# Shorter zero matmuls in three pauses of the head, and a new written-out order, in a fused attention and MLP kernel

## The chip, the cores and the metric

The kernel runs on one core of a Trainium2 chip. The metric is the device time of one execution in microseconds (us). The profiler also gives the span of a profiled execution, from its first to its last recorded instruction or transfer. Engines are named as in the profile: PE (TensorE matmuls), PEld (its weight loads), DVE (VectorE), ACT (ScalarE), POOL (GpSimd) and SP (SyncE, which issues nearly all DMAs here).

## The reference, cut to what matters

A transformer block on one sequence of S = 2048 tokens of width D = 448, in bf16. Six modulation vectors come from a condition vector; attention has 16 heads of 28 channels, and each query sees 8 keys at a stride of 2 tokens; the MLP is 1792 wide.

```python
mod = (silu(c) @ w_mod).reshape(1, 6, 1, 448)
sa, ca, ga, sb, cb, gb = (mod[:, i] for i in range(6))
h = layernorm(x) * (1 + ca) + sa
x = x + ga * (local_attention(h, wqkv) @ wo)      # 8 keys, dilation 2
h = layernorm(x) * (1 + cb) + sb
y = layernorm(h)
x = x + gb * (gelu(y @ w1 + b1) @ w2 + b2)
```

## The kernel before, in words

The tokens are split into two streams (even and odd, so that the dilated window becomes a dense one), and into 8 blocks `p` of 128 rows by 2 streams. A block is normalised on DVE, transposed (by PE for blocks 0 to 3, task names `tr0` to `tr3`; by DMA for 4 to 7, `zT4` to `zT7`), and scaled into `hT`. Blocks are projected to Q and K in units `[0] [1] [2,3] [4,5] [6,7]` (tasks `qk0`, `qk1`, `qk2`, `qk4`, `qk6`, each in halves `_0` for Q and `_1` for K and pieces `a` and `b`). Attention goes in nine batches `i` of 114 queries: V projection `v`, logits `lt`, exp on ACT, a mask multiply on DVE, denominators `pd`, weighted values `po`, a division on DVE (`omul`). Then per block an output projection `wo`, two layernorms on DVE, a DMA transpose `yT`, and per pair of blocks an MLP with tasks `w1`, gelu on ACT, `w2`, a final addition `fin` on DVE and a store.

Every step is a task with a number, added by `add` to a `Plan`. Nothing is scheduled while the kernel runs: `ORDER`, a text of 677 entries, gives the order in which the tasks are emitted, and so the order of instructions in each engine's own stream, which each engine executes strictly in that order. An entry `83:A` puts task 83 on ACT, `:D` on DVE, `:P` on POOL; `:R` picks the other way of a PE task, in which the quarter-depth matmuls (64 rows deep, line 534) come first and the full-depth ones (line 528) last. `SLOTS` gives each buffer its place; the four PSUM places (2 banks each) are reused all the time, so that a PE task also waits for the engine that reads the place's previous content. SP's loads keep one fixed order among themselves.

An entry `53+11@53` calls `filler(11, task 53)` ahead of task 53: that many matmuls of zeros on PE (line 370), written to the PSUM place that task 53 will overwrite. There are four such entries in the order before: ahead of 53 (`c_cols`, which turns the condition vector into columns), 69 (`mod_cols`), 85 and 91 (first pieces of `qk0`).

Numbers used below: 68 is `tr0`, 106 `tr1`, 128 `tr2`, 138 `tr3`, 164 `v0`, 209 `v1`, 114 and 115 the pieces of `qk1_1`, 111 and 112 those of `qk1_0`, 151 `mods` (line 599), 173 `po0`. On the other engines: 119 to 132 are statistics of blocks 2 and 3 (lines 433 and 435), 177 to 190 of blocks 4 and 5, 244 to 257 of blocks 6 and 7; 125, 126, 135, 136 the normalisations of blocks 2 and 3 (line 453); 107 to 110 the evictions of `tr1` into `hT` (lines 477 and 479); 165 and 210 the evictions of `v0` and `v1` (line 678 on ACT, 681 on DVE); 168 and 171 the masks of batch 0 (line 708); 663, 667, 671 and 675 the last additions (line 849) and 664, 668, 672 and 676 their stores.

Of the kernel before, what the change touches and what calls it, by code (L numbers as in the profile page):

```python
# [14 lines left out]
S, D, H, DH, F = 2048, 448, 16, 28, 1792  # L15
# [26 lines left out]
ENGINE = {"A": "ACT", "D": "DVE", "P": "POOL", "R": "PE2"}  # L42
RATE = 310e3
SLOTS = [
# [5 lines left out]
]  # L50
ORDER = """
0 4 16 1 2 3 8 17 14 13 15 18 9 6 19 11 12 7 20 5 10 21 61 53+11@53 22 59 23 54 62 60 55 63 56 57 64 58 65 66 24 67 25
68+14@69 69 26 27 77 71 70 28 72 78 73 74 29 76 75 85+9@85 82 86 30 97 80:A 31 91+3@91 92 83:A 99 93 32 84:A 98 81:A
79 94 100 95:R 101 33 129 102 87 103 88 96 104 89:R 34 131 105 35 121 106 90 36 132 164 130 122 119 37 109:A 133 108
134 110 169 107 165 166 120 38 136 209 123 254 170 124 256 167 135 39 114 257 125 255 137 244 115:R 126 245 40 210:D
127 138 116 128 258 189 259 111 141:A 41 246 112:R 190 139:A 171 168 140:A 42 151 247 261 113 248 179 43 249 173 142
152 44 214 180 260 211 45 251 215 148 250 177 262 46 212 216 153 263 178 252:A 187 172 276 181 174 150:D 182 175 253
188 184 143 191 183 213 277 176 185 192 218 186 145:D 217 147 219 194 193 47 220 195 154 144:R 48 149 221 196 311
146:D 266:A 49 265 117 50 264 278 312 118 313 51 267 281 279 528 52 272 564 282 157 280 314 529:R 159 274 155 283 269
199:A 156 200:A 315 198:A 161 222 271 162 163 530 197 284 160 285 286 419 202 223 287 158 201:R 288 204 226 289 224  # L60
203 227 225 228 229 205 290 231 293 206:R 207 230 294 291 232 316 208 292 346 233 295 317 236 296 234 351 347 318 348
268 298 349 235 297 237 299 352 350 320 270 300 319 273 238 353 321 301 239 303 322 354 302 241 420 304 275 240 305
323 242 306 356 243 355 455 421 324 307 308 357 309 310 456 381 358 325 359 457 326 328 397 327 360 329 382:R 361 398
363 399 362 330 364 331 365 366 387 333 384 367 368 383 332 369 385 334 386 370 335 392:R 390 373 400 401 389 336 388
374 338 404 391 337 371 403 339 372 340 375 422 396 408 376 393 395 341 394 406 377 418 343 342 378 409 405 379:A
344:A 380 423 402 425 461 426 458 345 424 407 459 427 414 462 410 463 411 415 460 465 464 428 466 412 430 413 467 431
565 468 491 416 429 507 566 417 432 492:R 509 508 469 495 496 493 433 470 494 510 514 471 497 511 473 434 513 474 472
435 512 437 502:R 436 475 438 500 476 439 498 440 499 501 478 442 441 477 515 505 443 503 479 444 504 517 480 506 447
527 483 516 481 484 445 531 570 482 448 532 534 446 485 518 449 486 571 533 523 535 487 572 536 524 519 450 537 488
520 538 452 539 451 567 489:D 453:D 521 490 568 540 569 454 522 541 573 574 525 575 542 576 526 616 600 543 577 601:R  # L70
618 544 617 546 545 547 548 549 578 550 603 551 602 552 604 606 619 623 579 605 622 582 580 620 583 581 584 553 611:R
607 585 556 609 554 610 621 557 555 608 558 587 586 559 626 612 588 615 560 614 632 589 613 561 590 562:A 627 592 563
591 593 594 624 595 597 596 625 598 599 633 628 630 629 631 651 634 635 641:R 652 653 636 645 644 643 642 646:R 637
638 654 656 640 639 658 655 661 647 649 657 650 659 648 662 660 665 663 664 666 669 667 670 668 673 671 672 674 675
676
"""


# [73 lines left out]
def kernel(  # L152
# [14 lines left out]
    nc = tc.nc  # L167
# [56 lines left out]
    warm_w = cst.tile([128, 256], BF16, name="warm_w")  # L224
# [142 lines left out]
    def filler(n, t):  # L367

        for _ in range(n):
            nc.tensor.matmul(t.sums[0].t[:, 0, 0:256], lhsT=warm_w[:, 0:128], rhs=warm_w[:, 0:256], start=True, stop=True)  # L370


    psc = psum("ps_c")
# [490 lines left out]
    for pi, (batches, tiles) in enumerate(PHASES):  # L864
# [18 lines left out]
        if pi < len(PHASES) - 1:  # L883
            tbl = add("ACT", 1.28, lambda: nc.scalar.preload_act_table_set(EXP_SET), after=list(gelus), name="tbl")
    P.emit(filler)

# [28 lines left out]
```

## Time and profile before

| | |
|---|---|
| median of 3 runs (lowest, highest) | 172.77 us (172.54, 174.36) |
| the profiled execution, its own time | 172.62 us |
| its span | 170.6 us |
| PE busy | 165.6 us (97%) |
| DVE busy | 115.7 us (68%) |
| ACT busy | 104.9 us (62%) |
| POOL busy | 42.0 us (25%) |
| matmuls recorded | 2152, of these 37 of zeros |

Rows of a chain or timeline begin with the start and the duration in us. A row that merges several instructions (x6) gives the time from the first start to the last end. What stands in brackets is the idle time of the engine just ahead of the row, and what ended it. Matmul durations are latencies: consecutive ones overlap, so the distance between two starts is shorter than one duration. Rows of groups give the total busy time and the mean of one instruction in ns.

### The profile page before, as it was taken

How to read it: one execution, taken by the hardware profiler on the slowest of the kernel's cores; microseconds unless marked ns; L12 is line 12 of the kernel's file. 1: busy time of each engine (PE TensorE's matmuls, PEld its weight loads, DVE VectorE, ACT ScalarE, POOL GpSimd, SP SyncE). 2: the span in 40 equal slices, each digit the busy share in tenths (PEclk: the TensorE clock that was granted, in tenths of full speed). 3: DMA queues.
4: the chain of work that ended last, by engine and by line, in shares of the span. 5: the costliest groups of instructions: out<-in, count | busy, mean ns of one | idle time of the engine just before them, and what ended most of it. 6: DMA issues, size and time to landing. Idle time of an engine off the chain costs nothing.

```text
span 170.6 us, 4990 instructions
## 1 busy us (share of the span) xinstructions
PE 165.6 (97%) x2152; PEld 84.3 (49%) x2152; DVE 115.7 (68%) x289; ACT 104.9 (62%) x144; POOL 42.0 (25%) x64
## 2 busy tenths in 40 slices
PE   7989999999999999999999999999999999999993
PEld 5856564453445454435555343555534455444562
DVE  6687999799989969897445168966689952200041
ACT  3278688679947995758939455866772920258200
POOL 6003132300011220499000057030018620007200
PEclk9999999999999999999999999999999999999999
DMA  5999999998000033000740100006600034100011
GB/s 157 317 319 316 261 244 291 156 259 248 6 0 4 6 62 67 0 0 0 63 121 0 58 0 0 0 4 88 147 4 2 0 65 115 56 0 0 0 58 54
DMA packets 20708, 15.12 MB, mean 89 GB/s; under 512 B 13705, under 2 KB 19726, under 8 KB 20686
## 3 DMA queue, kind: packets, MB, share of 16 engines
q1 hardware_dynamic: 20684, 14.80, 36.1%
q8 instruction: 17, 0.28, 0.7%
q14 instruction: 5, 0.04, 0.1%
q10 hardware_dynamic: 2, 0.00, 0.0%
HBM read 9.81 MB, written 1.84 MB: 68 GB/s over the span
## 4 chain that ended last, share of the span: by engine, by line
PE 86%; DMA 7%; DVE 2%; SPq 2%; issue 0%
PE p L843 25%; PE p L528 22%; PE pq L528 11%; PE pw L760 7%; DMA x_all<-in_A_x_dram 4%; PE p L534 4%; PE lt L695 3%; PE po L728 3%; DMA wm_st<-in_w_mod_dram 3%; PE pv L528 3%; PE pv L663 3%; PE pq L534 2%; PE pd L717 1%; DVE stt L433 1%; SPq L329 1%; SPq L325 1%
## 5 line engine op out<-in xcount | busy, mean ns | idle before, releaser
L821 ACT ACTIVATE hm<-p,b_col 128x512 bf16<-128x512 f32 x56 | 34.4, 687 | 30.0 <-PE p L534 23.1
L843 PE MATMUL p<-w_s,hm 128*128 128x448 bf16 (+1 forms) x238 | 43.8, 342 | 0.0
L528 PE MATMUL p<-yT,w_s 128*128 128x512 bf16 x168 | 38.6, 380 | 0.0
L843 PEld LDWEIGHTS <-hm 128*128 128x128 bf16 x238 | 22.8, 98 | 19.1 <-issue 0.3
L449 POOL TENSOR_TENSOR rs_all<-tv_all,neg_half 128x2 f32<-128x2 f32 x22 | 15.8, 724 | 60.9 <-DVE tv_all L447 54.1
L528 PEld LDWEIGHTS <-w_s 128*128 128x128 bf16 x168 | 15.7, 98 | 20.9 <-issue 3.4
L849 DVE TENSOR_TENSOR x_all<-p,x1p 128x896 bf16<-128x896 f32 (+2 forms) x10 | 9.0, 902 | 23.9 <-PE p L843 23.9
L528 PE MATMUL pq<-hT,Wqk 128*128 128x512 bf16 (+1 forms) x108 | 22.6, 345 | 0.4 <-DVE vb L681 0.4
L433 DVE BATCH_NORM_STATS2 stt<-x_all 128x6 f32<-128x448 bf16 x32 | 18.6, 613 | 2.1 <-DMA x_all<-in_A_x_dram 1.9
L702 ACT ACTIVATE et<-lt 128x928 bf16<-128x928 f32 x18 | 16.0, 946 | 1.2 <-PE lt L695 1.2
L798 POOL TENSOR_TENSOR x1p<-x_all,gbb_bc 128x448 f32<-128x448 bf16 x16 | 16.6, 1064 | 0.1
L708 DVE TENSOR_TENSOR et<-et,mask 128x928 bf16<-128x928 bf16 x18 | 11.2, 634 | 4.9 <-ACT et L702 4.9
L745 DVE TENSOR_TENSOR qT<-po,den 128x912 bf16<-128x912 f32 x9 | 10.0, 1106 | 6.6 <-ACT den L739 5.2
L528 PEld LDWEIGHTS <-Wqk 128*128 128x128 bf16 x108 | 9.4, 97 | 9.9 <-issue 3.5
L760 PE MATMUL pw<-wo_s,qT 128*128 128x448 bf16 x64 | 13.3, 353 | 0.0
L737 ACT ACTIVATE den<-pd 128x928 f32<-128x928 f32 x9 | 8.5, 954 | 7.8 <-PE pd L717 7.8
L767 DVE TENSOR_TENSOR x_all<-pw,x_all 128x896 bf16<-128x896 f32 x8 | 8.6, 1081 | 6.8 <-PE pw L760 6.8
L825 POOL COPY seen<-hm 128x1 bf16<-128x1 bf16 x4 | 3.2, 788 | 34.9 <-ACT hm L821 34.9
L776 DVE TENSOR_TENSOR h<-h,mod_bc 128x896 bf16<-128x896 bf16 x16 | 10.3, 672 | 0.1
L588 ACT CAST kT<-pq 128x1024 bf16<-128x1024 f32 x7 | 7.1, 1011 | 4.5 <-PE pq L528 2.4
L739 ACT ACTIVATE den<-den,den_bias 128x928 f32<-128x928 f32 x9 | 9.5, 1069 | 0.2
L433 DVE BATCH_NORM_STATS2 stt<-h 128x6 f32<-128x448 bf16 x16 | 9.2, 610 | 0.0
(101 smaller groups left out, 186.3 us busy)
## 6 DMA issues: line engine op xcount, KB each, us to landing
wmod<-in_w_mod_dram SPq DMA_DIRECT2D x4, 392.0 KB, 10.7
w_s<-in_B_w_dram SPq DMA_DIRECT2D x7, 224.0 KB, 5.2
out_dram<-x_all SPq DMA_DIRECT2D x7, 224.0 KB
x_all<-in_A_x_dram SPq DMA_DIRECT2D x3, 448.0 KB
w_s<-in_B_w_dram SPq DMA_DIRECT2D x3, 448.0 KB, 4.3
wqk_st<-in_A_wqkv_dram SPq DMA_DIRECT2D x3, 225.0 KB
wm_st<-in_w_mod_dram SPq DMA_DIRECT2D x1, 588.0 KB
x_all<-in_A_x_dram SPq DMA_DIRECT2D x2, 224.0 KB
```

The lines of the kernel that those rows point to most:

```text
L433: add("DVE", 0.53, lambda: nc.vector.bn_stats(out=stt[:, w, b, :], in_=src()), reads=reads, bufs=bufs, after=early if w == b == 0 else (), ...
L449: add("POOL", 0.55 + 0.17 * n, lambda: nc.gpsimd.tensor_tensor(out=r, in0=tv, in1=neg_half[:, 0:n], op=ALU.pow), reads=[f"tv{w}_{b0}", "ne ...
L528: nc.tensor.matmul(out(), lhsT=lhs(kt, slice(0, 128)), rhs=rhs(kt, slice(0, 128)), start=first and kt == 0, stop=not first and kt == KT - 2)
L534: nc.tensor.matmul(out(), lhsT=lhs(KT - 1, rows), rhs=rhs(KT - 1, rows), start=first, stop=not first, tile_position=(rows.start, 0))
L702: exps.append(add("ACT", 0.83, lambda half=half, lt=lt: nc.scalar.activation(out=et.t[:, 2 * half:2 * half + 2].rearrange("p r m c -> p r ...
L708: nc.vector.tensor_tensor(out=ev, in0=ev, in1=mask[:], op=ALU.mult)
L745: nc.vector.tensor_tensor(out=qT[:, :, LEAD + q00:LEAD + q00 + 2 * WQ], in0=po.t[:, :, 0:NS * 4 * WQ].rearrange("p j (m c) -> p m j c", c=WQ),
L760: nc.tensor.matmul(pw.t[:, s, 0:D], lhsT=qT[:, NS * PLACE[ft] + s, LEAD + 128 * p:LEAD + 128 * p + 128], rhs=wo_s[:, ft, :], start=(ft == ...
L776: add("DVE", 0.55, lambda vec=vec, op=op: nc.vector.tensor_tensor(out=h2.t[:], in0=h2.t[:], in1=vec.unsqueeze(1).to_broadcast([128, NS, D] ...
L798: add("POOL", 1.0, lambda n=n: nc.gpsimd.tensor_tensor(out=x1p.t[:, n, :], in0=xn(p, n), in1=gbb2_bc[:], op=ALU.add), reads=[f"x{p}", "gbb ...
L821: gelus.append(add("ACT", 0.585, lambda f=f, a=a, p1=p1s[g]: nc.scalar.activation(out=hm.t[:, f].rearrange("p n c -> p (n c)"), in_=p1.t[: ...
L843: nc.tensor.matmul(p2.t[:, n, 0:c1 - c0], lhsT=hm.t[:, f, n, q * 128:(q + 1) * 128], rhs=w2_s[:, f, c0:c1], start=(f == parts[0][0]), stop ...
```

## The change

The zero matmuls get 128 columns in place of 256. They stand ahead of tasks 53 (20 in place of 11), 69 (19 in place of 14) and 85 (18 in place of 9); the 3 ahead of task 91 are gone: 57 in place of 37, with 7296 columns in place of 9472. `ORDER` and `SLOTS` are new as a whole. The set of tasks is the same; 95 changes of the array's mode along PE's stream become 91 (mode: rows by columns of the tile that a matmul uses, as full, 64x128, 128x64 or 64x32). Of the diff, the heads and the ends of the order:

```diff
-0 4 16 1 2 3 8 17 14 13 15 18 9 6 19 11 12 7 20 5 10 21 61 53+11@53 22 59 23 54 62 60 55 63 56 57 64 58 65 66 24 67 25
-68+14@69 69 26 27 77 71 70 28 72 78 73 74 29 76 75 85+9@85 82 86 30 97 80:A 31 91+3@91 92 83:A 99 93 32 84:A 98 81:A
-79 94 100 95:R 101 33 129 102 87 103 88 96 104 89:R 34 131 105 35 121 106 90 36 132 164 130 122 119 37 109:A 133 108
-134 110 169 107 165 166 120 38 136 209 123 254 170 124 256 167 135 39 114 257 125 255 137 244 115:R 126 245 40 210:D
-127 138 116 128 258 189 259 111 141:A 41 246 112:R 190 139:A 171 168 140:A 42 151 247 261 113 248 179 43 249 173 142
...
-638 654 656 640 639 658 655 661 647 649 657 650 659 648 662 660 665 663 664 666 669 667 670 668 673 671 672 674 675
-676
+0 4 16 1 2 13 8 17 14 15 18 3 9 6 19 12 7 20 11 5 10 21 61 53+20@53 22 59 23 54 62 60 55 63 56 57 64 58 66 65 24 67 25
+68+19@69 69 26 27 77 71 70 28 72 78 75 74 29 76 73 82 30 85+18@85 86 99 83:A 31 91 80:A 92 97 32 93 84:A 100 81 94 98
+79 95:R 101 33 119 102 87 103 88 96 104 89:R 34 121 105 35 129 106 90 36 122 164 120 130 131 37 108:A 187 109:A 132
+123 110 169 124 165 107 166 38 256 209 170 126 246 167 257 39 133 177 114 134 210 179 168 115:R 40 135 125 111 116 189
+127 136 112:R 41 190 247 137:A 254 138 188 180 113 255 178 128 191 171 42 151 181 192 139:A 140 43 142 173 141:A 182
...
+654 646:R 657 653 652 656 640 658 655 665 650 649 647 659 648 669 661 670 662 671 672 660 673 663 666 664 674 667 675
+668 676
...
-            nc.tensor.matmul(t.sums[0].t[:, 0, 0:256], lhsT=warm_w[:, 0:128], rhs=warm_w[:, 0:256], start=True, stop=True)
+            nc.tensor.matmul(t.sums[0].t[:, 0, 0:128], lhsT=warm_w[:, 0:128], rhs=warm_w[:, 0:128], start=True, stop=True)
```

More of the change, by code (lines that the diff above doesn't have):

```diff
@@ L56 @@
-127 138 116 128 258 189 259 111 141:A 41 246 112:R 190 139:A 171 168 140:A 42 151 247 261 113 248 179 43 249 173 142
[L57 to L70, printed above, removed]
@@ L71 @@
-618 544 617 546 545 547 548 549 578 550 603 551 602 552 604 606 619 623 579 605 622 582 580 620 583 581 584 553 611:R
-607 585 556 609 554 610 621 557 555 608 558 587 586 559 626 612 588 615 560 614 632 589 613 561 590 562:A 627 592 563
-591 593 594 624 595 597 596 625 598 599 633 628 630 629 631 651 634 635 641:R 652 653 636 645 644 643 642 646:R 637
-638 654 656 640 639 658 655 661 647 649 657 650 659 648 662 660 665 663 664 666 669 667 670 668 673 671 672 674 675
-676
+0 4 16 1 2 13 8 17 14 15 18 3 9 6 19 12 7 20 11 5 10 21 61 53+20@53 22 59 23 54 62 60 55 63 56 57 64 58 66 65 24 67 25
@@ new lines @@
+68+19@69 69 26 27 77 71 70 28 72 78 75 74 29 76 73 82 30 85+18@85 86 99 83:A 31 91 80:A 92 97 32 93 84:A 100 81 94 98
+79 95:R 101 33 119 102 87 103 88 96 104 89:R 34 121 105 35 129 106 90 36 122 164 120 130 131 37 108:A 187 109:A 132
+123 110 169 124 165 107 166 38 256 209 170 126 246 167 257 39 133 177 114 134 210 179 168 115:R 40 135 125 111 116 189
+127 136 112:R 41 190 247 137:A 254 138 188 180 113 255 178 128 191 171 42 151 181 192 139:A 140 43 142 173 141:A 182
+244 44 214 152 258 245 211 193 45 215 311 184 183 153 194 212 46 216 47 172 248 259 195:A 312:D 185:A 143 174 249 186
@@ new lines @@
+175 213 144:R 260 145 250 176 196 218 251 261 217 252:A 146:D 148 219 253 262:D 220 147:R 150:D 263 221 117 276 149
+118 197 199:A 154 200 48 198 281 49 277:D 278 282 201 50 51 419 279 283 52 264 266:A 205:R 280 203 156 265:A 155 284
+285 158 207 222 157 286 160 161 267:A 202 162 287 223 528:A 269:R 288 204 224 289 226 271 225 159 227 163 272 290 228
+293 229 346 274 291 294 231 230 316 292 347 232 313 206 295 233 314 296 236 317 234 273:R 208 297 235 237 298 238 315
+348 299 275 351 268 318 349 300 239 352 303 319 301 529 270 350 241 321 302 353 320 455 530 354 304 240 355 305 356
@@ new lines @@
+242:D 306 420 243 322 308 307 357 456:R 323 309 310 421 564 324 358 381 457:D 359 325 397 360 326 382:R 361 399 327
+328 398 362 363 329 364 330 365 331 387 366 385 383 333 368 386 367 332 384 369 334 392:R 388 370 391 335 373 400 389
+401 338 390 374 371 403 339 406 336 394 405 372 337 375 396 340 393 408 402 395 341 418 422 425 404 461 423 409 342
+462 343 424 412 426 344 463 345 376 414 427 377 428 378 429 379:D 430 380 413 431 458 415 459 432 407 460 416 464 465
+410 466 417 433 411 467 502 491 434 468 437 435 492:R 438 506 436 439 505 440 503 441 504 442 443 497 444 495 494 447
@@ new lines @@
+496 445 448 493 446 449 450 565:R 498 510 513 501 500 469 451 452 566 512 453:A 507 499 511 454 470 514 473 521 509
+471 508 474 472 475 527 476 534 570 567 478 523 535 477 479 571 536 531 568 480 524 572 532 483 522 569 484 533 573
+525 574 575 538 481 537 526 576 515 482 485 486 539 577 516 540 487 488 517 600 541 489:A 578 490 542 579 580 518 582
+581 543 606 519 544 520 546 545 583 601:R 547 584 607 548 585 608 549 610 609 587 551 550 586 616 603 552 602 588 553
+605 611:R 589 618 554 619 617 622 590 604 592 621 556 620 593 591 632 555 557 613 594 558 615 595 612 630 559 614 596
@@ L76 @@
+597 633 561 560 623 562:A 626 563 598 599 624 625 631 627 634 641 628 635 629 636:R 644 642 645 643 651 638 637 639
+654 646:R 657 653 652 656 640 658 655 665 650 649 647 659 648 669 661 670 662 671 672 660 673 663 666 664 674 667 675
+668 676
 """
```

10 rows, old and new, of the table SLOTS are left out of this document.

## The prediction

> **What bounds the kernel now.** I read the page first, then the chain that ended last, then the timeline of the first 25 us by engine. The page:
>
> ```profile
> span 170.6 us, 4990 instructions
> PE 165.6 (97%) x2152; PEld 84.3 (49%) x2152; DVE 115.7 (68%) x289; ACT 104.9 (62%) x144; POOL 42.0 (25%) x64
> PE 86%; DMA 7%; DVE 2%; SPq 2%; issue 0%
> ```
>
> PE is busy 97% of the span and makes up 86% of the chain. The windows say where PE ever runs dry and how full DVE is there (columns of the windows: length, then busy time with the instruction count for PE, PEld, DVE, ACT and POOL):
>
> ```profile
> 18.00:22.00 4.00, 3.58 (x38) 2.51 (x36) 4.00 (x13) 2.55 (x4) 1.32 (x3) 1.00 1.02 239
> 26.00:40.00 14.00, 14.00 (x253) 6.08 (x251) 12.86 (x27) 10.92 (x15) 2.17 (x4) 1.00 1.14 238
> 40.00:60.00 20.00, 20.00 (x341) 9.02 (x338) 19.23 (x45) 16.51 (x20) 2.39 (x3) 1.00 0.10 33
> ```
>
> In 18 to 22 PE is idle for 0.42, then in the whole of 26 to 60 for nothing, and the list of waits has none of PE behind 22 either. So a new order can shorten that stretch only by making PE's own stream shorter, and can lengthen it by any single late input. The chain, with the head's longest piece and the last ones:
>
> ```profile
> 9.84 7.61 DMA x_all<-in_A_x_dram
> 17.48 1.15 DVE stt L433 x2
> 18.63 0.30 DVE zy L453
> 18.93 0.09 DVE mvs L435
> ...
> 167.66 0.39 DVE x_all L849
> ```
>
> The last step is an addition on DVE (block 7). In the head the end is set by a load of x (blocks 6 and 7), which lands at 17.46, then by DVE's list behind it, statistics, normalisations and the eviction of `v1`.
>
> **The zero matmuls.** They stand in gaps that other things end:
>
> ```profile
> 1.12 2.53 PE L370 MATMUL ps_c<-warm_w 128*128 128x256 bf16 x11 [1.12 <-DVE warm_w L240]
> 4.02 2.38 PE L370 MATMUL ps_col<-warm_w 128*128 128x256 bf16 x14
> 6.24 0.61 PE L510 MATMUL ptr<-ident,zy 128*128 128x128 bf16 x8
> 6.68 1.32 PE L398 MATMUL ps_col<-silu_bc,wm_st 112*128 112x32 bf16 x40
> 7.93 1.16 PE L370 MATMUL pq<-warm_w 128*128 128x256 bf16 x9
> 8.92 0.60 PE L550 MATMUL pq<-hT,Wqk 128*128 128x256 bf16 x4
> L370 PE MATMUL ps_c<-warm_w x11: 393/421/421, 1.1 to 3.2; 128*128 128x256 bf16 x11
> L370 PE MATMUL pq<-warm_w x12: 272/272/283, 7.9 to 9.6; 128*128 128x256 bf16 x12
> ```
>
> The first eleven start at 1.1 to 3.2, so 0.21 us apart for 256 columns, 0.107 us for 128: twenty of 128 take 2.1 us, 0.2 less than eleven of 256. The nine of the third pause take from 7.93 to 8.92, 0.11 us each; eighteen of 128 at half of that, 0.055, take the same 1.0 us. The nineteen take between 1.05 us (all at 0.055) and 2.0 us (all at 0.107) where fourteen took 2.2. So all three groups end with or ahead of the ones before, and what ends the pauses is not theirs: the condition vector, the normalised block 0, the scaled block 0. The three dropped stood between the first pieces of `qk0`, in a pause that ends with DVE's copy of the K weights. Cost and gain of this part: 0; bounds -0.1 (if the third group held `qk0` up) and the price of a slow clock (second rival).
>
> [...] The row: one zero matmul takes 421 ns at first and 272 ns in the last pauses. [...]
>
> **The mode changes.** Their price is read where the same six matmuls stand with and without one ahead:
>
> ```profile
> 40.77 1.29 PE pq L528 x6
> 42.07 0.32 PE pq L534 x2
> ...
> 46.28 0.54 PE pq L534 x4
> 46.82 1.40 PE pq L528 x6
> ```
>
> Six full ones behind others of full mode take 1.29, behind 64-row ones 1.40. Two 64-row ones cost 0.32, four cost 0.54, so 0.22 for two and 0.10 for the change. Four changes fewer (95 to 91, all of it between `tr1` and the first `w1`, 55 to 51, and one fewer and one more later): 4 x 0.1 = -0.4 us. Bounds: -0.45 and 0, the latter if PE waits there anyway.
>
> **The head.** The new stream of PE behind `tr1` is `v0`, `lt0`, `v1`, `qk1_1`, `qk1_0`, then `tr3`, `tr2`, `mods`; before, the transposes stood ahead of `qk1_0`. The eviction of `v1` goes from DVE to ACT. On DVE, statistics of blocks 4 and 5 (187) and 6 and 7 (256) come earlier, 187 even ahead of the evictions 110 and 107 that `v1` needs. The rows of before:
>
> ```profile
> 9.21 1.10 SPq L329 DMA_DIRECT2D x_all<-in_A_x_dram  x2
> 11.63 0.63 DVE L433 BATCH_NORM_STATS2 stt<-x_all 128x6 f32<-128x448 bf16 x1 [0.38 <-DMA x_all<-in_A_x_dram]
> 14.62 1.05 DVE L477 TENSOR_SCALAR hT<-ptr,mod_col 128x256 bf16<-128x256 bf16 x3
> 16.29 1.64 PE L663 MATMUL pv<-Wv,hT 128*64 128x448 bf16 x16
> 17.86 0.83 PE L528 MATMUL pq<-hT,Wqk 128*128 128x256 bf16 x6
> 19.61 1.29 PE L510 MATMUL ptr<-ident,zy 128*128 128x128 bf16 x16
> 21.32 0.82 PE L528 MATMUL pq<-hT,Wqk 128*128 128x256 bf16 x6 [0.42 <-DVE vb L681]
> 23.15 0.94 PE L599 MATMUL pb<-wmod,silu_bc 112*32 112x448 bf16 x16
> Wv<-in_A_wqkv_dram SPq DMA_DIRECT2D x1, 336.0 KB, 5.3
> x_all<-in_A_x_dram SPq DMA_DIRECT2D x3, 448.0 KB
> ```
>
> When x of blocks 4 and 5 lands no row says. Between the landing of blocks 2 and 3 (11.63) and of 6 and 7 (17.46), SP's order has the V weights (336 KB and two small pieces, together some 450 KB), blocks 4 and 5 (448 KB), blocks 6 and 7 (448 KB). Three equal shares of 5.83 us put it at 15.5, an estimate; bounds 14.6 (it makes nobody wait) and 17.46.
>
> DVE's list is the same work as before up to 14.6 (the statistics of blocks 2 and 3 and two normalisations, in another order), then the wait to 15.5, 187 to 16.05 (0.53 each when back to back: 1.15 for two, less the overlap), a small pair 0.15, two evictions at 1.05/3 = 0.35 each: 16.9. So `v1` starts at 16.95 in place of 16.29: 0.65 late. `v1` takes 1.57 (16.29 to 17.86), `qk1_1` 1.75 (17.86 to 19.61), `qk1_0` 1.83 (21.32 to 23.15): PE is at 22.1 then. `tr3` needs 136, the last normalisation. Ahead of it behind 17.48 stand five statistics (2.65), four normalisations (0.29 each, 1.16), two small ones (0.16) and a mask (0.56): 22.0, and its tail copy on ACT (0.3) ends at 22.35. `tr3` and `tr2` take 0.95 (16 of 0.055 and the issue): `mods` starts at 23.35 in place of 23.15. The waits of before (0.42 for the eviction, 0.3 inside the transposes) are gone, two others stand in their place. Term: +0.2. Bounds: -0.2 (DVE's list 0.4 faster; then `qk1_0` ends last), +1.5 (x at 17.46: 187 to 18.0, then 0.85, and the list of 4.5 behind that: 23.4, `tr3` at 23.7, `mods` at 24.65).
>
> Nothing is behind that to absorb or add: up to `omul` of batch 4, DVE loses an eviction of `v1`, one of `qk2`, a few of `hT` (3.5 us together) and gains the evictions of `v2` and `v3` and some of `hT` (3.6 us): 0.
>
> **The tail.** Before, the last piece of PE is followed by one addition and its store. In the new order the addition of block 7's first stream (667) comes with only a 6-matmul piece behind its inputs, so two additions and two stores end together.
>
> ```profile
> L849 DVE TENSOR_TENSOR x_all<-p,x1p 128x448 bf16<-128x448 f32 x1 | 0.6, 625 | 1.6 <-PE p L843 1.6
> 166.74 1.67 SPq L853 DMA_DIRECT2D out_dram<-x_all  x2
> 166.79 0.83 PE L843 MATMUL p<-w_s,hm 128*128 128x224 bf16 x7
> ```
>
> The piece takes some 0.57 (6 of the 0.1 at which the last 7 follow each other, within 0.83), the addition 0.625: 0.1 late; SP then issues two stores behind each other, the first while the last addition (0.39) runs. By the row of the last two issues, 1.67 with a wait for the last addition in it, one issue is between 0.4 and 0.8, so the last store waits 0 to 0.4 more for its turn. Term +0.2; bounds 0 and +0.5.
>
> **The sum.** 172.62 (the profiled execution's own time: span 170.6 and 2.0 around it) + 0 - 0.4 + 0.2 + 0.2 = 172.6, no change. The median of the runs is 172.77, 0.15 above that execution; the forecast for a median is 172.8. Its own range by the bounds, which do not all fall together: 172.0 to 174.0.
>
> **Rivals.**
>
> First, slower: DVE is late for `po0`. From 17.48 the new list holds, up to and with the second mask of batch 0 (171), six statistics, four normalisations, nine small ones and two masks. With overlap (0.53, 0.29, 0.08, 0.56) that is 6.2 us, done at 23.7, and `po0` is due at 24.2. The means of the groups are longer:
>
> ```profile
> L433 DVE BATCH_NORM_STATS2 stt<-x_all 128x6 f32<-128x448 bf16 x32 | 18.6, 613 | 2.1 <-DMA x_all<-in_A_x_dram 1.9
> L708 DVE TENSOR_TENSOR et<-et,mask 128x928 bf16<-128x928 bf16 x18 | 11.2, 634 | 4.9 <-ACT et L702 4.9
> L435 DVE BATCH_NORM_AGGREGATE mvs<-stt 128x2 f32<-128x6 f32 x48 | 7.3, 168 | 0.0
> L453 DVE TENSOR_SCALAR zy<-x_all,mvs,rs_all 128x448 bf16<-128x448 bf16 x16 | 5.6, 379 | 0.1
> ```
>
> Without overlap, by these means, the list is 8.0 us, done at 25.5: 1.3 late, and the evictions 140 and 142, which `lt1` and `v3` need, come behind it. It decides from 0.5 us of lateness on. For it: DVE is full from 18 to 22 and 96% full from 40 to 60. Against it: the chain shows the overlap (0.30 and 0.09 where the means say 0.38 and 0.17). With 0.2 more for the tail: 172.8 + 1.6 = 174.4. Chance 0.20.
>
> Second, slower: the clock. If PE stays at half rate past 6.2 us, `tr0` takes twice its 0.4 (6.24 to 6.68) and the modulation columns up to twice their 1.3 us (6.68 to 7.95): 0.4 to 1.7 late, 173.2 to 174.5. [...] Chance 0.06.
>
> Third, faster: the load of x lands early and DVE's list keeps ahead, so that both of the head's new waits vanish (another 0.6) and the tail costs nothing (0.2): 172.8 - 0.2 - 0.6 - 0.2 = 171.8; with the mode changes costing a little more, 171.5. It can't be much more, since PE has only 0.4 of idle time behind 11 us. For it: the order before lost its time at just this load. Against: the wait at 17.46 stands in both. Chance 0.12.
>
> **How the numbers follow.** The forecast has 0.62, the rivals 0.20, 0.06 and 0.12. 1% of 172.77, about what a measurement of this kernel can tell from no change, is 1.73: 171.04 and 174.50. Slower by more: 0.09 from the first rival, 0.03 from the second, 0.08 from the forecast's upper bound where DVE or the load is later than worked out: 0.20. Faster by more: a third of the third rival, and little else: 0.06. Within: 0.74. The range takes in both rivals' times: 171.4 to 174.8.
>
> **What would show it.** `v1` starting 0.4 to 0.9 late with a wait for DVE ahead; `mods` at 23.2 to 23.6; PE without idle time from there to its end; PE's stream from `mods` to its last matmul 0.4 shorter; the end 0.2 longer behind the last matmul. Wrong if PE shows idle time over 0.3 us behind 25 us, or if the mean of the third pause's matmuls shows the slow clock.

## The result, and the profile after

| | us |
|---|---|
| changed kernel, median of 4 runs (lowest, highest) | 175.31 (175.2, 175.5) |
| kernel before, beside it, median of 4 runs | 173.0 (172.54, 174.36) |
| ratio, with its 95% interval | 1.0109 [1.0062, 1.0157] |
| the profiled execution: its own time, its span | 175.34, 173.6 |
| forecast (range) | 172.8 (171.4 to 174.8) |

The change is slower by 1.1%, and the time lies above the range: the medians are 2.3 us apart, the two profiled executions 2.7 (172.62 and 175.34). The kernel before varied between 172.1 and 177.7 on the chips used later, so experiments are compared by their ratio to the runs of it on the same chip; runs in which the chip was in a slower state are left out of the ratios (five of the ten of e2 and five of the twelve of f2 among them), and the profiles of f1 and h3 fell in it.

The page of the changed kernel; of the queues, q8 is taken for the one of TensorE's instructions, since its 17 packets fit their number (below):

```profile
span 173.6 us, 5023 instructions
PE 165.4 (95%) x2172; PEld 84.9 (49%) x2172; DVE 118.3 (68%) x291; ACT 105.3 (61%) x146; POOL 42.4 (24%) x60
q8 instruction: 17, 0.28, 0.7%
PE 82%; DMA 10%; DVE 4%; issue 1%; SPq 1%
```

PE's busy time is 0.2 us less than before (165.6), the span 3.0 us longer: PE now stands idle, which the prediction excluded behind 22 us. Four of the eight rows of PE's waits in the changed kernel (what PE waited for, total, count, longest); the other four lie ahead of 18 us:

```profile
PE pd L717 <- issue: 1.5, 1, 1.5
PE pw L760 <- DVE w_s L617: 0.6, 1, 0.6
PE ptr L510 <- DVE zy L453: 0.4, 1, 0.4
PE pq L370 <- DVE mod_col L410: 0.3, 1, 0.3
```

The longest has "issue" as its cause: no semaphore, no engine and no transfer that the profile shows. The timeline of PE around it, in the changed kernel:

```profile
112.97 2.44 PE L843 MATMUL p<-w_s,hm 128*128 128x448 bf16 x12
115.35 0.39 PE L717 MATMUL pd<-et,ones_k 64*32 64x464 bf16 x8
115.55 1.29 PE L728 MATMUL po<-et,vb 64*32 64x57 bf16 x128
116.66 0.38 PE L717 MATMUL pd<-et,ones_k 64*32 64x464 bf16 x3
118.53 0.38 PE L717 MATMUL pd<-et,ones_k 64*32 64x464 bf16 x5 [1.49 <-issue]
118.84 4.33 PE L843 MATMUL p<-w_s,hm 128*128 128x448 bf16 x22
```

and of the same batches in the kernel before:

```profile
116.33 0.39 PE L717 MATMUL pd<-et,ones_k 64*32 64x464 bf16 x8
116.54 0.73 PE L728 MATMUL po<-et,vb 64*32 64x57 bf16 x64
117.20 0.44 PE L695 MATMUL lt<-qT,kT 28*64 28x58 bf16 x32
117.58 2.82 PE L843 MATMUL p<-w_s,hm 128*128 128x448 bf16 x14
120.33 0.39 PE L717 MATMUL pd<-et,ones_k 64*32 64x464 bf16 x8
120.54 0.73 PE L728 MATMUL po<-et,vb 64*32 64x57 bf16 x64
```

The new order has `pd8`, `po8`, `po7` and `pd7` in one run of 144 short matmuls, with as many weight loads, in 1.5 us; before, long `w2` matmuls stood in between. In the midst of `pd7`, whose eight matmuls have the same inputs ready, PE stops behind the third. Eight matmuls of `pd` take 0.20 us from start to start (115.35 to 115.55), 0.025 each, so the third starts at 116.71; the fourth starts at 118.53, **1.8 us** late. (The 1.49 in brackets is counted from the modelled end of the third.) The DMA transfers of two adjoining stretches of the changed kernel, 115 to 115.9:

```profile
DMA packets 0, 0.00 MB, mean 0 GB/s; under 512 B 0, under 2 KB 0, under 8 KB 0
```

and 115.9 to 118.6 (queue, packets, MB, share of 16 engines):

```profile
q8 instruction: 1, 0.02, 2.4%
```

A packet of PE's instructions is fetched there. The trace has it from 115.97 to 117.02, so PE goes on 2.6 us behind its start and 1.5 us behind its end; what happens between the end of the transfer and PE's next matmul no view shows. The page counts 17 such packets for 4344 matmuls and weight loads, some 256 instructions each.

TensorE's last matmul, one of `w2`, starts 2.9 us later than before. How much of that lies where is read from the `w2` matmuls (min, median and max duration in ns, then first and last start), before:

```profile
L843 PE MATMUL p<-w_s,hm x238: 259/352/363, 78.3 to 167.4; 128*128 128x448 bf16 x105, 128*128 128x224 bf16 x14
```

and after:

```profile
L843 PE MATMUL p<-w_s,hm x238: 259/352/363, 78.8 to 170.3; 128*128 128x448 bf16 x105, 128*128 128x224 bf16 x14
```

From first to last it was 89.1, it is 91.5: **+2.4**, of which the stop is 1.8. Ahead of it, PE's timeline of the changed kernel has `v1`, `mods` and the first `wo`:

```profile
17.70 1.64 PE L663 MATMUL pv<-Wv,hT 128*64 128x448 bf16 x16
22.77 1.06 PE L510 MATMUL ptr<-ident,zy 128*128 128x128 bf16 x16
23.75 0.56 PE L599 MATMUL pb<-wmod,silu_bc 112*32 112x448 bf16 x8
42.82 1.69 PE L760 MATMUL pw<-wo_s,qT 128*128 128x448 bf16 x8 [0.59 <-DVE w_s L617]
```

`mods` is 0.6 late (23.15 before), and `wo0` waits 0.6. From `mods` to the first `w2` it was 55.15, it is 55.05: without that wait 0.7 shorter than before, and the 0.6 of the 2.4 that the stop doesn't explain is mostly work that the new order has moved behind the first `w2`: 32 more matmuls of `lt` (256 against 224) stand there, and the new order without a stop, below, has 0.5 more in this stretch.

### The profile page after: what moved, and what is told of

Read it like the earlier page. It is cut to its first block, busy times and chain, and to the rows that moved or that the text cites. A ratio compares the mean times of both kernels' runs of the same rounds, so it can differ in the third digit from the quotient of the medians.

```text
span 173.6 us, 5023 instructions
## 1 busy us (share of the span) xinstructions
PE 165.4 (95%) x2172; PEld 84.9 (49%) x2172; DVE 118.3 (68%) x291; ACT 105.3 (61%) x146; POOL 42.4 (24%) x60
## 3 DMA queue, kind: packets, MB, share of 16 engines
HBM read 9.81 MB, written 1.84 MB: 67 GB/s over the span
## 4 chain that ended last, share of the span: by engine, by line
PE 82%; DMA 10%; DVE 4%; issue 1%; SPq 1%
PE p L843 25%; PE p L528 21%; PE pq L528 9%; PE pw L760 7%; PE p L534 4%; DMA x_all<-in_A_x_dram 4%; DMA mod_bc<-mod_hbm 3%; DMA wm_st<-in_w_mod_dram 3%; PE lt L695 3%; PE pv L528 3%; PE pv L663 3%; PE po L728 3%; PE pq L534 2%; PE pd L717 2%; DVE stt L433 1%
## 5 line engine op out<-in xcount | busy, mean ns | idle before, releaser
L843 PE MATMUL p<-w_s,hm 128*128 128x448 bf16 (+1 forms) x238 | 44.3, 342 | 0.0
L449 POOL TENSOR_TENSOR rs_all<-tv_all,neg_half 128x2 f32<-128x2 f32 x22 | 17.8, 816 | 84.4 <-DVE tv_all L447 84.3
L453 DVE TENSOR_SCALAR zy<-h,mvs,rs_all 128x448 bf16<-128x448 bf16 x16 | 8.5, 567 | 3.9 <-POOL rs_all L449 3.8
L776 DVE TENSOR_TENSOR h<-h,mod_bc 128x896 bf16<-128x896 bf16 x16 | 9.4, 620 | 0.1
```

What stands on the lines that cost most here:

```text
L449: add("POOL", 0.55 + 0.17 * n, lambda: nc.gpsimd.tensor_tensor(out=r, in0=tv, in1=neg_half[:, 0:n], op=ALU.pow), reads=[f"tv{w}_{b0}", "ne ...
L843: nc.tensor.matmul(p2.t[:, n, 0:c1 - c0], lhsT=hm.t[:, f, n, q * 128:(q + 1) * 128], rhs=w2_s[:, f, c0:c1], start=(f == parts[0][0]), stop ...
```

## The experiments

What separates the theories is **which** of the change's parts is slower: the order, the short zero matmuls, or only both together. "The stretch" below is from the first to the last start of a `w2` matmul (89.1 before, 91.5 after); the expectations count to the last one's end, 0.2 to 0.3 more.

**The parts alone, first set.** The new order with the old zero matmuls, the old order with the new ones, and the new order with 37 short ones. In these three the second group stands behind `tr0`, ahead of 69, while in both kernels it stands ahead of task 68, which is `tr0`, and writes the place of 69 (so the line on the four entries, above, is to be read). The first set is therefore not quite the parts alone; the second is.

```diff
-61 53+20@53 ... 68+19@69 69 ... 85+18@85 ... 31 91 80:A
+61 53+11@53 ... 68 69+14@69 ... 85+9@85 ... 31 91+3@91 80:A     (e1, 256 columns)
+61 53+20@53 ... 68 69+19@69 ... 85+18@85                        (e2, in the old order)
+61 53+13@53 ... 68 69+13@69 ... 85+11@85                        (e3, 128 columns)
```

> The new order and places with the old zero matmuls (256 columns, 11, 14, 9 and 3 of them, at the old tasks). Theory A (PE's instruction stream): the 20 zero matmuls more of the change, with their 20 weight loads, bring every later fetch of PE's instructions 40 instructions earlier in the program; the fetch at 116 us then falls into the run of 288 short instructions of pd8, po8, po7, pd7, and PE stands for 1.49 us without any engine to wait for. With 37 in place of 57 the stop at pd7 is gone and the end is about 1.5 us earlier; the load of x of blocks 2 and 3, which lands at 13.3 in place of 11.6, lands at 11.6 again, another 0.4 to 0.6: some 173.2 to 173.9 in all. Theory B (the order alone): pd7 waits in its place for the addition 525 on DVE, whatever stands in the head, and the head's loss is DVE's list: the stop stays at 1.4 to 1.5 us and the time at 175.0 to 175.4.

> The old order and places with the new zero matmuls (128 columns, 20, 19 and 18). Theory A: every later fetch comes 40 instructions earlier in the program; by the old trace only one stretch is as dense (po6, pd6, pd5 at 87 us and lt8, pd, po at 116 to 121), so a stop is possible but small, 0 to 0.7 us; the load of x of blocks 2 and 3 lands later than 11.6, by up to 1.7, which this order feels by 0.3 to 0.6: 172.9 to 174.0. Theory B: the zero matmuls lie in pauses that others end and cost nothing: 172.6 to 173.0.

> The new order with short zero matmuls (128 columns), 37 of them (13, 13 and 11) in place of 57: as many instructions as the old filling, but 4736 columns in place of 9472. Theory A (the count of instructions): as with the old filling, the stop at pd7 is gone, 173.2 to 173.9. Theory B: 175.0 to 175.4. A third, the array's clock: with fewer columns PE stays at the slow clock longer, the third pause's matmuls show over 300 ns, and qk0 starts 0.3 to 1.5 us later: 175.5 to 177.

Measured: 0.9986 [0.9945, 1.0027], 1.0001 [0.9957, 1.0046] and 1.0004 [0.9971, 1.0037]. No ratio is clear of 1, but e2's profile has a wait that the kernel before has not (see f2, below). In e1 and e3, `pd7` has no stop, and the stretch is 89.6 in both. e1's `qk0` starts at 10.76, 1.8 us later than before, and yet `mods` starts at 23.36: the loads of x and DVE set the end of the head, not PE's fillers. In e3 the slow rate of the first zero matmuls (0.107 us for 128 columns) lasts longer: the last four transposes of `tr0` take 0.63 there (all eight took 0.61 before), and `qk0` starts at 11.46, 0.7 behind e1; its ratio shows no price of that.

**The parts alone, placed right.**

```diff
-61 53+20@53 ... 68+19@69 69 ... 85+18@85 ... 31 91 80:A
+61 53+11@53 ... 68+14@69 69 ... 85+9@85 ... 31 91+3@91 80:A     (f1, 256 columns)
```

f2 is the kernel before with `53+20@53`, `68+19@69`, `85+18@85` and 128 columns.

> The new order and places with the old zero matmuls, each group at its old place (the second ahead of tr0). Theory A (PE's instruction stream): the stop at pd7 (1.49 us in the changed kernel) is gone, since each fetch comes 40 instructions later in the program; the load of x of blocks 2 and 3 lands at 11.6 and not at 13.3, as the first fetch of PE's instructions comes behind it; mods starts at 23.0 to 23.4 in place of 23.75: about 1.5 to 2.0 us below the changed kernel on the same chip, within 0.5 us of the kernel before. Theory B (the order alone): the stop stays and the time is that of the changed kernel.

> The old order and places with the new zero matmuls, each group at its place. Theory A: the first fetch comes at about 10.4 and not 11.8, so x of blocks 2 and 3 lands 1.5 us later and this head loses 0.3 to 0.6; behind it a stop wherever 160 or so instructions behind a fetch are short ones: po and pd at 24, 31, 57, 61, 87 and 117 us; 0 to 0.7: 0.3 to 1.2 us above the kernel before. Theory B: no difference beyond 0.2 us.

> The changed kernel once more, on the chip on which the others of this group run, so that they can be compared with it. Both theories: its stop of 1.3 to 1.5 us at pd7 and its time of 1.0 to 1.2% above the kernel before are there again.

Measured, on one chip: f1 0.997 [0.9934, 1.0007], f2 1.002 [0.9979, 1.006], the changed kernel itself (f4) 1.0203 [1.0163, 1.0243], above the 1.0 to 1.2% that was expected of it. Neither part alone shows the loss in its ratio, though f2's interval reaches 1.006. PE's timeline of f1 at `pd7`:

```profile
116.72 1.29 PE L728 MATMUL po<-et,vb 64*32 64x57 bf16 x128
117.83 0.42 PE L717 MATMUL pd<-et,ones_k 64*32 64x464 bf16 x8
118.18 4.34 PE L843 MATMUL p<-w_s,hm 128*128 128x448 bf16 x22
```

The same dense run, unbroken. f2 has no stop there either, but its stretch is 91.0 (90.9 in e2), 1.9 more than before, by another wait. SP's queue and PE's timeline of f2:

```profile
117.68 3.54 SPq L790 DMA_TRANSPOSE yT<-zy  x2
124.89 1.46 PE L527 MATMUL p<-yT,w_s 128*128 128x512 bf16 x6 [1.68 <-DMA yT<-zy]
```

and the same matmuls in the kernel before:

```profile
122.72 1.46 PE L528 MATMUL p<-yT,w_s 128*128 128x512 bf16 x6
```

The transposes of `y` are issued 0.3 later than before (117.36) and hold PE up by 1.7 (by 1.6 in e2). A packet of PE's instructions began 1.0 us behind their issue before (118.37); it begins 0.3 behind it in f2 (117.95) and together with it in e2 (118.72). Whether this is what makes them late, no run settles, and since f2's runs lie between 172.21 and 176.55 us, the wait need not be in every one. So in these two profiles the new zero matmuls go with a loss in the old order too, whose cause is open; the stop at `pd7` is seen only where the new order and the larger number meet.

The changed kernel differs from f1 in its zero matmuls alone: they are shorter, and more of them. 20 zero matmuls more are 40 instructions more (each has a weight load: the pages count 2172 of both, 2152 before), so that a load of instructions that ends at a fixed count ends 40 instructions earlier in the program. The changed kernel stands behind 3771 recorded instructions, in the dense run; in f1 that count lies 20 matmuls behind the third of `pd7`, among long `w2` matmuls.

**The place of the stop, by the count.** Theory A: an instruction load ends at a fixed count, and PE stands if what it still has of the load before runs out ahead of it.

```diff
-53+20@53 ... 68+19@69 ... 85+18@85
+53+20@53 ... 68+19@69 ... 85+26@85      (f5: 8 more)
+53+14@53 ... 68+13@69 ... 85+18@85      (f6: 12 fewer)
```

> The changed kernel with 26 in place of 18 zero matmuls in the third pause: 16 instructions more ahead of all else. Theory A: the fetch that comes too late brings the instructions from a fixed count on, so the stop moves 16 instructions, 8 matmuls, ahead: out of the third matmul of pd7 and into the last 5 to 10 matmuls of po7 (line 728), with 1.4 to 1.6 us. Theory B (pd7 waits for its place, or for an input): the stop stays at the same matmul of pd7, whatever stands in the head.

> The changed kernel with 45 zero matmuls of 128 columns (14, 13 and 18) in place of 57, otherwise as it is. Theory A (TensorE's instructions come 256 at a time, and TensorE stands where such a load falls into a dense run of short instructions): 12 matmuls fewer are 24 instructions fewer, so the load that stopped TensorE inside pd7 stands 24 instructions later in the program, 12 matmuls further on: behind pd7, in the first or second w2 piece. The stop of 1.3 to 1.7 us inside pd7 is gone or at most 0.3 us, pd7 is one row of eight, the ratio to the kernel before is 0.995 to 1.006. Theory B (the new order itself is slower there, or 57 zero matmuls delay the head whatever their number): the stop stays inside pd7, or the ratio stays at 1.01 to 1.02.

PE's timeline of f5:

```profile
118.43 1.25 PE L728 MATMUL po<-et,vb 64*32 64x57 bf16 x123
119.95 0.21 PE L728 MATMUL po<-et,vb 64*32 64x57 bf16 x5 [0.27 <-issue]
119.97 0.39 PE L717 MATMUL pd<-et,ones_k 64*32 64x464 bf16 x8
```

and of f6:

```profile
117.20 0.42 PE L717 MATMUL pd<-et,ones_k 64*32 64x464 bf16 x8
117.55 1.50 PE L843 MATMUL p<-w_s,hm 128*128 128x448 bf16 x7
119.57 3.01 PE L843 MATMUL p<-w_s,hm 128*128 128x448 bf16 x15 [0.52 <-issue]
```

Eight more: the stop stands ahead of the last 5 of `po7`, that is 5 and the 3 of `pd7`, eight matmuls earlier. Twelve fewer: behind the 5 left of `pd7` and 7 of `w2`, twelve later. No input changes with that number, so a wait for data is out. Seven long matmuls at 0.2 us cover 1.4 of the 1.8; what is left in f6 is 0.67 (a gap of 0.87 between starts, less 0.2), more than the 0.3 expected; its packet also began 0.4 later, 0.28 ahead of `pd7` where that of the changed kernel began 0.69 ahead. f6: 1.008 [1.0019, 1.0142], above the range expected; stretch 90.3, and another 1.2 of "issue" in `po1` ahead of it. The single run of f5 took 177.03 us: the late stop was only 0.27 (1.5 was expected), but the profile has 1.9 of "issue" ahead of a `qk2` piece at 31.1 and 1.3 of a late `yT`. Its load began 0.8 us ahead of `po8`, that of the changed kernel 0.4 behind; why, is not known.

The count fits every "issue" wait in the traces of this case, 26 in 17 profiles. Counted from the start, 703, 959 (957 in e2), 1471 or 3771 of PE's recorded matmuls and weight loads stand ahead of the wait, in either order and whatever matmul comes next: steps of 256, of 512 and of 2300, and nine times 256 is 2304. Each of these waits ends 2.3 to 2.9 us behind the start of the latest packet of PE's instructions and 1.3 to 1.6 us behind its end. So the count sets the place of a stop, and the start of the packet its length.

**The count alone.** The strongest test: the order and the long zero matmuls of f1, which were not slower, with 20 nearly empty matmuls added.

```diff
 def filler(n, t):
+    for _ in range({11: 9, 14: 5, 9: 6, 3: 0}[n]):
+        nc.tensor.matmul(t.sums[0].t[:, 0, 0:16], lhsT=warm_w[:, 0:128], rhs=warm_w[:, 0:16], ...)
     for _ in range(n):
```

> The new order with the 37 zero matmuls of 256 columns of the kernel before, and 20 more of 16 columns added to the same groups (9, 5 and 6, ahead of the long ones): TensorE's instructions stand at the numbers they have in the changed kernel, the clock's work is that of the kernel before. Theory A (the count decides where an instruction load falls): a stop of 1.3 to 1.8 us inside pd7 in front of its fourth matmul, the stretch from the first w2 matmul to TensorE's last one 91.5 us or more (89.9 with 37 zero matmuls), ratio 1.006 to 1.016. Theory D (short zero matmuls or their clock are the cause): no stop there, 89.9 us in that stretch, ratio 0.995 to 1.002.

> The changed kernel, beside the others on the same chip. All theories: ratio 1.010 to 1.020, the stop in front of pd7's fourth matmul, 91.5 us or more from the first w2 matmul to TensorE's last one.

Measured, on one chip: h1 1.017 [1.0117, 1.0222], the changed kernel 1.0163 [1.0107, 1.0218]. PE's timeline of h1 (lines moved by 2):

```profile
117.69 0.38 PE L719 MATMUL pd<-et,ones_k 64*32 64x464 bf16 x3
119.54 0.38 PE L719 MATMUL pd<-et,ones_k 64*32 64x464 bf16 x5 [1.47 <-issue]
```

The stop is back, behind the same third matmul, with the long zero matmuls of the kernel before; the stretch is 91.4. Theory A holds, and the columns have no part in this stop. The ratio is just above the 1.016 that was expected at most; what the stop doesn't explain of it lies ahead of the stop, where `wo0` waits 1.6 in its profile.

**Taking the stop away at the same count.** One `w2` piece (task 515; it has 8 matmuls, not the 22 and 7 of the expectations) is moved into the dense run: between `po8` and `po7` (g2), between `po7` and `pd7` (i1), there with `mod_bc` early (i2). h4 was meant as i1, but leaves 515 behind `pd7` (task 537), so that PE's stream is the changed kernel's.

```diff
-525 574 575 538 481 537 526 576 515 482
+525 574 575 515 538 481 537 526 576 482     (g2)
+525 574 575 538 481 537 515 526 576 482     (h4)
+525 574 575 538 481 515 537 526 576 482     (i1, i2)
```

> The changed kernel with all 57 zero matmuls of 128 columns; one w2 piece (22 long matmuls, task 515) moved from behind pd7 to between po8 and po7, so that the run of 288 short attention matmuls is broken in its middle. Theory A: the load of TensorE's instructions starts within 160 instructions of the same place and now runs during long matmuls: no stop over 0.3 us in this stretch. Something is lost where the w2 piece now stands (its inputs, or the output place that po7 wants, up to 0.7 us), so 0.6 to 1.5 us net come back: ratio 1.002 to 1.010, 0.6 to 1.5 us less than the changed kernel. Theory B (pd7 waits for data or a place that the profile doesn't show): the stop stays with pd7, 1.3 to 1.7 us.

> The changed kernel with all 57 zero matmuls; the w2 piece behind pd7 (task 515, 7 long matmuls, 1.5 us) moved to between po7 and pd7, so that no wait for po7's place can come of it. Theory A: the instruction load starts at the same place and has 1.5 us more of cover: the stop is 0 to 0.5 us, the stretch from the first w2 matmul to TensorE's last one 90.0 to 90.6 us, and the time 1.0 to 1.8 us below the changed kernel beside it. Rival (the time goes into waits of the batch's division, which pd7 now feeds 1.5 us later, ahead of wo): 91 us or more although the stop is gone.

> The changed kernel with all 57 zero matmuls; the w2 piece behind pd7 (task 515, 1.5 us of long matmuls) moved to between po7 and pd7 (537). Theory A: the instruction load starts where it started and has 1.5 us more of cover, so TensorE stands 0.2 to 0.7 us in place of 1.8; the stretch from the first w2 matmul to TensorE's last one is 90.1 to 90.7 us in place of 91.6 to 91.9; the ratio to the kernel before is 0.006 to 0.009 below the changed kernel's 1.011 to 1.020, so 1.003 to 1.013. Rival (TensorE's later waits absorb what is won): 91.3 us or more in that stretch, as with the first way of spacing.

> The same with mod_bc's load issued ahead of the DMA transpose of block 6. Theory A with the second cause (mod_bc behind four transposes makes wo0 0.6 to 1.8 us late): no wait for w_s ahead of wo0, the stop as in the other, ratio 0.998 to 1.006. If mod_bc's place is worth nothing, as the other one.

Measured: g2 1.0145 [1.0088, 1.0202], h4 1.0222 [1.0166, 1.0278], i1 1.0115 [1.0064, 1.0166], i2 1.0082 [1.0052, 1.0112]. PE's timeline of g2:

```profile
118.12 1.67 PE L843 MATMUL p<-w_s,hm 128*128 128x448 bf16 x8 [0.52 <-ACT den L737]
119.72 0.68 PE L728 MATMUL po<-et,vb 64*32 64x57 bf16 x64
120.21 0.42 PE L717 MATMUL pd<-et,ones_k 64*32 64x464 bf16 x8
123.91 0.36 PE L760 MATMUL pw<-wo_s,qT 128*128 128x448 bf16 x1 [0.53 <-DVE qT L745]
```

and of i1:

```profile
116.69 0.73 PE L843 MATMUL p<-w_s,hm 128*128 128x448 bf16 x3
118.52 1.12 PE L843 MATMUL p<-w_s,hm 128*128 128x448 bf16 x5 [1.10 <-issue]
123.28 3.20 PE L760 MATMUL pw<-wo_s,qT 128*128 128x448 bf16 x16 [0.56 <-DVE qT L745]
```

In g2 the stop is gone. In i1 it keeps its place in the count: behind the third matmul after `po7`, which now is a `w2` one, for 1.25 us (a gap of 1.45, less 0.2). Only these 3 of the 8 stand ahead of it, 0.6 us of cover, and 0.6 came off; the expectation had counted the whole piece. But the time did not come back: `po7` or `pd7` come later, the division feeds `wo` 0.5 later, and g2's new piece waits 0.5 besides. The stretch is 91.1 in g2, 91.9 in i1. g2 and i2 lie above their ranges; i1's ratio lies within its own, but its stretch is what its rival said, that later waits absorb what is won. h4 keeps the stop, as the changed kernel's PE stream must.

**The place of `mod_bc`.** In the changed kernel SP's queue and DVE's timeline show what `wo0` waits for:

```profile
28.27 7.28 SPq L502 DMA_TRANSPOSE zT<-zy  x4
35.64 0.53 SPq L608 DMA_DIRECT2D mod_bc<-mod_hbm  x1
```

```profile
41.13 1.16 DVE L611 TENSOR_TENSOR wo_s<-wo_s,mod_bc 128x896 bf16<-128x896 bf16 x2 [0.82 <-DMA mod_bc<-mod_hbm]
```

The load of the gates is issued behind all four DMA transposes; before, behind three, at 33.58.

```diff
-252:A 146:D 148 219 253 262:D ... 197 199:A 154 200
+252:A 146:D 148 219 154 253 262:D ... 197 199:A 200     (154 is mod_bc)
```

> The changed kernel with one move: SP issues the load of the modulation rows (154) ahead of the DMA transposes of blocks 6 and 7 instead of behind them. In the changed kernel it is issued at 35.6 and lands at 41.1, DVE's scaling of wo waits for it 0.82 us and PE's first wo 0.59 us. Theory: it is issued at about 32, lands by 37.5, PE's wait of 0.59 is gone, and the transposes of blocks 6 and 7 come 0.6 later without a wait: 0.4 to 0.6 us less, 174.7 to 174.9. Rival: the transposes become the late ones, or PE meets another late input right behind it: 175.1 to 175.5.

> The new order with the 37 zero matmuls of 256 columns of the kernel before (11, 14, 9 and 3, ahead of the same tasks), and the load of mod_bc (154) issued ahead of the DMA transpose of block 6 (253). Theory A: no stop of 1 us inside pd7, no wait of 0.6 us ahead of wo0, but up to 0.5 us behind the transpose issued later; against the new order with the old zero matmuls alone 0 to 0.6 us less: ratio 0.993 to 1.000 to the kernel before. Theory C (what the new order saves of mode changes and loses at mod_bc is real, and nothing else differs): 0.994. If mod_bc's place makes no difference, 0.997 as without.

> The new order with 37 zero matmuls of 128 columns (13, 13 and 11 ahead of 53, tr0 and 85: half the columns of the kernel before, the same number of TensorE instructions) and mod_bc's load issued early. Theory A: instruction loads stand where they stand with the 37 long ones, so no stop inside pd7; 0.993 to 1.003. Theory D (short zero matmuls leave the clock slow, or the order is slower with any short ones): 1.008 or more, with the head's first short matmuls at 300 ns or more for longer than in the changed kernel.

> The new order with the 37 zero matmuls of 256 columns and mod_bc's load issued early, once more: 0.990 to 0.999 of the kernel before; no stop inside pd7, 89.9 us from the first w2 matmul to TensorE's last one.

In e4 SP issues it at 32.11 and the wait of `wo0` is gone; the stop stays, and 0.5 of a late `yT` appears: 1.007 [1.0048, 1.0092]. What the move is worth can't be read from that ratio, as the changed kernel itself had 1.011, 1.016 and 1.020 on other chips. i2 beside i1 gives 1.0082 and 1.0115, with intervals that overlap, and 1.1 of a late mask in i2's profile. With the old zero matmuls: g1 0.9945 [0.989, 1.0], and again as h3 **0.9935 [0.9894, 0.9975]**, faster than both kernels (by 0.65% than the kernel before). Against f1 (0.997, on another chip) the intervals overlap, so that what the place of `mod_bc` is worth is not settled by times. g3, with 37 short ones, 1.0002 [0.9951, 1.0053]. The stretch of g1 is 89.7 and that of g3 89.6 (78.9 to 168.5); the `w2` row of g1:

```profile
L843 PE MATMUL p<-w_s,hm x238: 259/352/363, 77.6 to 167.3; 128*128 128x448 bf16 x105, 128*128 128x224 bf16 x14
```

The kernels of the new order in which no `w2` piece was moved into the dense run, by their zero matmuls:

| zero matmuls | kernels | stop near `pd7` (idle shown) | stretch |
|---|---|---|---|
| 37 of 256 | e1, f1, g1, h3 | none | 89.6 to 89.7 |
| 37 of 128 | e3, g3 | none | 89.6 |
| 45 of 128 | f6 | 0.52 | 90.3 |
| 57 of 128 | changed, e4, h2, h4 | 1.34 to 1.78 | 91.3 to 91.7 |
| 37 of 256 and 20 of 16 | h1 | 1.47 | 91.4 |
| 65 of 128 | f5 | 0.27 | 90.1 |

f4 had the stop too (1.69), and 93.4 in a profile with a granted clock of 0.99. "None" is said of `pd7` alone: with 37, "issue" waits of 0.2 to 1.9 us stand in `po0` or `po1` instead (e1, e3, f1, g1 and g3), ahead of the stretch.

## Why the prediction was wrong

- **The step that failed: "cost and gain of this part: 0"** for the zero matmuls, with "PE without idle time from there to its end". It counted their time on the array, which lies in pauses indeed, and not their number: 20 more shift all that follows in the instruction stream. In this order that costs 1.8 us at 117. The upper bound of that term, the price of a slow clock (0.4 to 1.7 us in the second rival), was an estimate of the author that no run shows: the granted clock was 1.000 in the profiles of both kernels, and in e3, where the slow rate lasted longer, the ratio was 1.0004. What the runs show in its place is the stop of 1.8 us, which no rival had. It was also taken for granted that only a late input can stop PE; the profile's own word for a wait without a releaser, "issue", stood at 0% in the page of before.
- **The sum of independent parts.** The order and the fill were priced each alone, and alone neither is clearly slower (0.997 and 1.002, the latter with a wait of 1.7 for a DMA transpose in its profile). The stop at `pd7` comes from both together, for which the sum had no term.
- **Nothing "behind that to absorb or add": wrong by 0.6 us** in the changed kernel's profile (1.2 and 1.8 in its two later ones). The balance of DVE's evictions was worked out, the SP queue was not, where the gates' load stood behind one transpose more.
- **The head: right in its kind, low in size.** `mods` at 23.75, forecast 23.35, bound 24.65. `v1` is 1.4 late, not 0.65. The forecast had x of blocks 2 and 3 as before at 11.63; DVE's timeline of the changed kernel has it later:

```profile
13.29 0.63 DVE L433 BATCH_NORM_STATS2 stt<-x_all 128x6 f32<-128x448 bf16 x1 [1.21 <-DMA x_all<-in_A_x_dram]
17.77 0.63 DVE L433 BATCH_NORM_STATS2 stt<-x_all 128x6 f32<-128x448 bf16 x1 [0.17 <-DMA x_all<-in_A_x_dram]
```

  Blocks 6 and 7 come at 17.75 or so, near the 17.46 assumed. PE's first instruction packet, earlier by the 40 instructions too, may hold this load up: of the nine profiles in which it begins by 10.7 us six have such a wait for x (0.88 to 1.84 us) and three have not (in f5 the packet comes as early and the statistics start at 11.38), and no profile with a later packet has it. Whether the packet is the cause is open.
- **The mode changes: -0.4 forecast, -0.1 left in the sum.** From `mods` to the last `w2` start it was 144.25, it is 146.55; less the stop (1.8) and the wait of `wo0` (0.6) that is 0.1 less than before. What the four changes are worth by themselves no run separates.
- **The tail: +0.2 forecast, +0.1 measured.** Two additions end together, as said, but DVE ends some 0.7 behind the last `w2` start in both (168.05 before). From that start to the end of the span, with the stores, it is 3.2 before and 3.3 after:

```profile
170.02 0.97 DVE L849 TENSOR_TENSOR x_all<-p,x1p 128x448 bf16<-128x448 f32 x2 [0.74 <-PE p L843]
```

- **The first rival** comes nearest to the measured time (174.4; its terms of 1.3 and 0.2 add up to 174.3), by luck: PE has no wait for DVE's masks at `po0` in its list. **The third** did not come: the statistics of blocks 6 and 7 start at 17.77, not early. **The second** is refuted: the zero matmuls of the third pause run at the fast rate (219 ns for 128 columns; at the slow rate they took 311 to 314), and `tr0` stands ahead of them, at 6.12, with 0.62 for its eight (0.61 before):

```profile
L370 PE MATMUL ps_c<-warm_w x20: 286/311/311, 1.1 to 3.1; 128*128 128x128 bf16 x20
L370 PE MATMUL ps_col<-warm_w x19: 219/314/314, 3.8 to 5.5; 128*128 128x128 bf16 x19
L370 PE MATMUL pq<-warm_w x18: 216/219/219, 8.2 to 9.1; 128*128 128x128 bf16 x18
```

Of the +2.9 us of PE's end: 0.6 head, 1.8 stop, 0.6 `wo0`, -0.1 the rest. That the stop stands where it does by the count is shown (h1, f5, f6, i1). That the time would come back at the same count is not: the three kernels that broke the run up lost much of what they won in new waits. The ratio of the changed kernel was 1.011, 1.020 and 1.016 on three chips; 1.8 us is 0.010 of it, and what the rest varies with isn't settled.

## What to carry to other kernels

Added instructions cost more than their time here: 20 nearly empty zero matmuls in the head shifted where the instruction loads fall and brought a stop of 1.47 us inside `pd7` (h1). So count instructions, not only microseconds, and look for runs of many short matmuls without a long one among them, as the 144 here. When an order is tuned, tune it with the final number of instructions, since an order that is good with 37 fillers lost 1.8 us with 57. A wait whose cause is "issue" in the midst of a task with all inputs there was the mark of it here, and the queue of the engine's instructions is the place to check.

## What the runs showed of the hardware

- TensorE's instructions come in packets of some 256: 17 packets for 4344 matmuls and weight loads, and stops 256, 512 or 2300 recorded instructions apart. The dense run did not hide such a load: 128 short matmuls and their 128 weight loads passed in 1.1 us (115.55 to 116.66), 4.3 ns each, and PE then stood 1.8 us.
- Long matmuls behind the dense run hid such a load about one for one, out of 1.8 us: 0.6 us of them in i1 left 1.25, 1.4 us in f6 left 0.67, with a packet that began 0.4 later.
- PE went on 2.3 to 2.9 us behind the start of a packet wherever it stood for one (26 waits), while the packet of `pd7` took 1.1 us itself.
- There is a second such place in the new order, behind 959 recorded instructions, in `po1` of most kernels: "issue" was 1.9 there in f1, 1.3 in g2, 1.2 in f6, 0.8 in g3, and nothing in the changed kernel's first profile. g1 and h3 are one kernel, with 0.4 there and nothing: whether a stop is seen at the same place differs between executions, which may be part of the kernel's spread.
